# Attention followed by routed experts on one core: the first batch's keys fetched ahead of its queries, in fewer transfers, and the second batch's q and k issued later

## Chip, core and metric

The kernel runs on one core of a Trainium2 chip. The metric is the device time of one execution in microseconds (us). Engines are named as in the profile: PE (matrix multiplication; PEld are its weight loads), DVE (vector), ACT (activation), POOL (GpSimd) and SP (which here only issues transfers). POOL and SP each issue transfers to a queue of their own, q0 for POOL and q1 for SP; both are served by the core's 16 DMA engines.

## What is computed

The attention takes q, k and v of shape (8 batches, 8 heads, 576 rows, 64). It is the sum of two attentions: one on rows averaged in fours (144 by 144 scores, repeated back to 576 rows) and one in a band of three rows either side. Its output, seen as 4608 rows of 512, goes through eight experts; each row goes to one of them.

```python
out_d = sm_attn(q_d, k_d, v_d)            # rows averaged in fours
mask = np.abs(pos[:, None] - pos[None, :]) < 4
out_local = softmax(where(mask, scale * q @ k.T, -1e9)) @ v
x = (np.repeat(out_d, 4, axis=2) + out_local)  # as (4608, 512)
e_idx = argmax(x @ w_gate)
out[mask_e] = gate_w * eom * (relu(x @ w1[e]) @ w2[e])
```

## The kernel before

**Units.** Attention works in 32 units u0 to u31, four for each batch; a unit is two heads. q and k of a batch come in four slots, a slot being two neighbouring heads: 128 partitions of nine rows each. The transfer converts float32 to float16. Slots 0 and 1 are needed together by the first pair of units (w = 0: u0 and u1), slots 2 and 3 by the second (w = 1). The second batch's q and k serve u4 to u7, the third batch's u8 to u11.

**Loads.** `load_qk` (L436 to L448) makes one POOL task for q and one for k. For the first batch it is called three times, for slot 0, for slot 1 and for slots 2 and 3 (L864), so that POOL issues q, k, q, k, q, k; for each later batch it is called once with all four slots. Two buffers each for q and k hold two batches, so the third batch's loads wait until the first batch's slots have been transposed. `load_v` (L452) makes four SP transfers of 80 KB for each unit; each is 64 partitions of five runs of 64 numbers, so 320 pieces of 256 bytes. v has five buffers: u0 to u4 are issued without waiting, u5 needs u0's buffer. The v of u0 goes out at once; that of u1 waits for the first group of k transposes (the dependency "q and k go first", and L881). Behind the v of u4, SP issues eight small transfers of the gate's weights, wg (L402), and only then the v of u5.

**Front of the pipeline.** For a pair of units `prep` (L473) transposes k and then q on PE (L487, 18 instructions each, "Tk" and "Tq" here); DVE and ACT copy them out (L499; both groups of q on DVE). POOL then adds neighbouring rows: ks and kd from k (L512, L521), qs and qd from q (L512, L515). For the first pair, POOL does each unit by itself: ks, kd, qs, qd of u0, then of u1; after that come ks, kd, qs, qd of w = 1. Behind these, POOL makes constants for the gate (`c_gate`, L410 to L417), and DVE has a task `c_rev` (L420 to L427) that reads them. DVE runs its instructions in program order, and `c_rev` stands ahead of the first unit's normalisation.

**A unit.** `means_v` (L531) averages v on PE (L380, called VD), ACT copies the means. `scores` (L549) makes the averaged scores (L560, DS) and the band scores (L573 and L583, LS) on PE, and ACT takes exponentials. `values` (L592) multiplies by v: V1 (L609, averaged), V2 (L618, sums), V3 (L630, band). ACT makes reciprocals (L643, L638, L646), DVE multiplies (L653, and L660 with L664: M1), POOL adds the two attentions (L670). In PE's order VD(u1) stands ahead of V1(u0), and VD(u5) ahead of LS(u3). A few products without use (`fill`, L1008) are put on PE where the planner sees a gap; four of them stand ahead of V1(u1) and write a tile that M1(u0) reads.

**What orders the work.** Every piece is a task with a planned duration, a slot number and a weight from a table. `order` (L118) simulates the engines and yields one sequence; `late` (L165) walks it and holds a task back until its dependencies, its buffers and, where set, the task named in its `behind` have been emitted. `behind` places tasks in an engine's queue by hand; for the head of the kernel these stand in L880 to L888:

```python
    for u in range(1, NU):
        for t in vb[u][1]:
            t.behind = st[0]["tk"]
    t_wg.behind = vb[3][1][-1]
    st[1]["e21"][1].behind = st[0]["e20"][0]
    st[2]["e21"][0].behind = st[1]["e20"][1]
    t_cg.behind = st[2]["e20"][0]
```

In these names `e20` is POOL's qs with qd and `e21` its ks with kd, indexed by the unit of the pair; `qb[b]["loads"][0]` lists the loads of slots 0 and 1, q first and k last. Before the change the second batch's loads have no `behind`: POOL issues q of the second batch after the first few constants and k after the band masks, both before any work on the first batch. Each engine runs its own queue in order, and semaphores hold it where data is missing.

Of the kernel before, what the change touches and what calls it, by code (L numbers as in the profile page):

```python
# [51 lines left out]
def _ap(t, ap_list, extra_off=0):  # L52
    return bass.AP(tensor=t.tensor, offset=t.offset + extra_off, ap=ap_list)
# [27 lines left out]
class Plan:  # L81
# [9 lines left out]
    def add(self, kind, slot, eng, dur, fn, deps=(), uses=(), mode=None, lat=0.0, dma=0.0):  # L91
        t = Task(kind, slot, eng, dur, fn, [d for d in deps if d is not None], list(uses), mode, lat, dma)
        for b in t.uses:
            b.users.append(t)
        for d in t.deps:
            d.next.append(t)
        self.tasks.append(t)
        return t
# [105 lines left out]
def kernel(  # L204
# [11 lines left out]
    nc = tc.nc  # L216
    B, H, S, D = q.shape
# [213 lines left out]
    qb, vb = {}, {}  # L431
# [4 lines left out]
    def load_qk(b, s0=0, s1=NP):  # L436
        if b not in qb:
            qb[b] = {"bufs": [Buf(r_qk[0]), Buf(r_qk[1])], "loads": {}}
        for i, src in enumerate((q, k)):
            buf = qb[b]["bufs"][i]  # L440

            def fn(buf=buf, src=src):
                nc.gpsimd.dma_start(buf.tile[:, s0:s1, :],
                                    _ap(src[b, 2 * s0], [[9 * D, 128], [2 * S * D, s1 - s0], [1, 9 * D]]))
            t = add("qk"[i] + "b" if b else "qk0", NP * (b - 1) if b else s0 - 9, "POOL", 0.84, fn, uses=[buf],
                    dma=0.95 * (s1 - s0))
            for s in range(s0, s1):
                qb[b]["loads"].setdefault(s // 2, []).append(t)  # L448
# [20 lines left out]
    st = {}  # L469
# [381 lines left out]
    def weights(e, part=None):  # L851
# [3 lines left out]
        for i, w in enumerate((moe_w1, moe_w2)):  # L855
# [4 lines left out]
            elif part // 2 == i:  # L860
                c = slice(part % 2 * n // 2, (part % 2 + 1) * n // 2)
                nc.gpsimd.dma_start(wts[e][i][:, c], src[:, c])

    for s in ((0, 1), (1, 2), (2, 4)):  # L864
        load_qk(0, *s)
    for b in range(1, B):
# [18 lines left out]
    for t in st[2]["tq"]:  # L885
        t.behind = st[0]["ds"]
    st[2]["e21"][0].behind = st[1]["e20"][1]
    t_cg.behind = st[2]["e20"][0]  # L888
    t_w = {}
    for e in range(3):  # L890
# [172 lines left out]
    def tiles():  # L1063
        return (sbF.tile([128, 4, 128 * CAPJ], F16, tag="xgT", name="xgT"),
                sbF.tile([128, NG, 128 * CAPJ], F16, tag="hs", name="hs"),
                sbF.tile([128, CAPJ, Dm], F32, tag="y", name="y"))

    with tc.manual_schedule():
# [8 lines left out]
        for e in range(E):  # L1077
            w1sb, w2sb = wts[e]
            xgT, hs, y = xts[e]
# [10 lines left out]
            for j in range(nj):  # L1090
                col = CAPJ * (E - 1 - e) + parts[e][1] + j
                down(xgs[e], hs, y, j, w2sb, sidx[:, col:col + 1], True)
                k = 1 if nj > 2 else 2
# [10 lines left out]
    with tc.If(v_most > 0):  # L1104
# [12 lines left out]
        for e in range(E):  # L1117
# [4 lines left out]
            with tc.For_i(0, n_more, 1):  # L1122
# [13 lines left out]
                xgT, hs, y = tiles()  # L1136
# [34 lines left out]
```

## Time and profile before

| | |
|---|---|
| median of 3 runs | 387.89 us (384.99 to 389.81) |
| the profiled execution | 390.27 us |
| its span, first to last instruction | 388.5 us |
| PE busy in the span | 333.7 us (86%) |
| POOL busy | 236.1 us (61%) |
| ACT, DVE busy | 199.9 us (51%), 194.6 us (50%) |
| mean granted clock of PE | 0.975 |

The profiled execution took 390.27 us, of which 388.5 us lie between its first and its last instruction and 1.77 us around them. Times of rows are counted from the first instruction. A PE that is busy by the profile is not PE at its peak, since matmuls are pipelined. A granted clock of 1.00 is the upper of PE's two levels (2.4 GHz), 0.50 the lower (1.2 GHz).

### The profile page before, as it was taken

Reading aid. Unit: us, or ns where it says so; the run is one execution under the profiler, and the core shown is the slowest. Engines: PE = TensorE matmul, PEld = TensorE weight load, DVE = VectorE, ACT = ScalarE, POOL = GpSimd, SP = SyncE. Lnnn points to the kernel's source line nnn. Section 1 sums busy time; section 2 is a strip of 40 time slices with the busy share of each in tenths; the row PEclk is TensorE's granted clock in tenths of the full one; section 3 lists DMA queues with packets and bytes.
Section 4 is the critical chain, followed back from the end, with each engine's and each line's share of the span. In section 5 each row is a group of like instructions: output and inputs, shape, how many; then the busy total and the mean of one; then the engine's idle time right before and its main releaser. Section 6 shows DMA issues by size and latency. Waiting matters only on the chain.

```text
span 388.5 us, 13050 instructions
## 1 busy us (share of the span) xinstructions
PE 333.7 (86%) x5542; PEld 236.7 (61%) x5542; DVE 194.6 (50%) x505; ACT 199.9 (51%) x421; POOL 236.1 (61%) x295
## 2 busy tenths in 40 slices
PE   1685998998778877888887889999999999999991
PEld 1564776786667665666675666555756565666650
DVE  4634357778466675657783767322334232323210
ACT  1346676687567775746776544234333334333431
POOL 8867396778475677556667361356766766752322
PEclk9999899999989999889999999999999999999997
DMA  8949359969797999857495131434999999980212
GB/s 137 211 75 188 71 103 153 191 146 165 149 173 125 166 179 165 157 105 136 96 167 109 36 93 47 137 119 111 194 253 259 242 264 224 236 241 29 94 56 81
DMA packets 75237, 57.12 MB, mean 147 GB/s; under 512 B 46493, under 2 KB 67485, under 8 KB 75168
## 3 DMA queue, kind: packets, MB, share of 16 engines
q0 software_dynamic: 26272, 40.92, 53.8%
q1 hardware_dynamic: 48896, 15.26, 18.3%
q8 instruction: 45, 0.74, 0.8%
q14 instruction: 24, 0.20, 0.2%
HBM read 68.21 MB, written 15.22 MB: 215 GB/s over the span
## 4 chain that ended last, share of the span: by engine, by line
PE 56%; issue 13%; DMA 9%; ACT 9%; DVE 5%; POOL 4%; SPq 1%; POOLq 0%; DVEq 0%; ACTq 0%
PE PL L609 8%; PE U L1048 6%; PE Y L1058 6%; PE S L618 4%; PE PL L974 4%; DMA v<-in_v_dram 4%; PE PL L630 4%; POOL out_dram L909 3%; PE PL L960 3%; PE T L487 3%; PE T L380 3%; PE T L834 3%; PE T L710 3%; DMA xg<-hx_xs,gidx 3%; PE S L560 2%
## 5 line engine op out<-in xcount | busy, mean ns | idle before, releaser
L1058 PE MATMUL Y<-w,hs 128*128 128x512 f16 x248 | 57.3, 379 | 0.0
L909 POOL DMA_INDIRECT out_dram<-y,sidx x31 | 30.7, 990 | 39.7 <-ACT y L1060 22.1
L1048 PE MATMUL U<-xgT,w 128*128 128x320 f16 (+1 forms) x384 | 51.9, 295 | 0.4 <-DVE hs L1053 0.4
L670 POOL TENSOR_TENSOR x<-xl,xd 128x576 f16<-128x576 f32 x32 | 39.8, 1247 | 18.8 <-DVE xl L664 15.1
L1053 DVE TENSOR_SCALAR hs<-U 128x320 f16<-128x320 f32 (+1 forms) x52 | 24.6, 476 | 51.6 <-PE U L1048 40.2
L1048 PEld LDWEIGHTS <-w 128*128 128x128 f16 x416 | 40.6, 98 | 16.0 <-issue 1.8
L1060 ACT ACTIVATE y<-Y,xg 128x512 f32<-128x512 f32 x31 | 21.2, 687 | 45.6 <-PE Y L1058 31.6
L904 POOL DMA_INDIRECT xg<-hx_xs,gidx x31 | 31.5, 1017 | 14.2 <-issue 7.9
L1058 PEld LDWEIGHTS <-hs 128*128 128x128 f16 x248 | 23.6, 98 | 24.3
L1051 ACT ACTIVATE hs<-U 128x320 f16<-128x320 f32 (+1 forms) x52 | 21.9, 424 | 28.0 <-PE U L1048 27.1
L609 PE MATMUL PL<-e,vd 64*128 64x144 f32 x384 | 35.6, 320 | 0.0
L521 POOL TENSOR_TENSOR kd<-ks 64x192 f16<-64x192 f32 x64 | 32.4, 523 | 2.3
L487 PE MATMUL T<-id,qk 128*64 128x128 f16 x576 | 25.8, 237 | 9.3 <-POOL gfirst L356 6.1
L512 POOL TENSOR_TENSOR ks<-kT 128x576 f32<-128x576 f16 (+1 forms) x17 | 18.6, 1093 | 24.5 <-ACT kT L499 22.2
L630 PE MATMUL PL<-e,v 64*64 64x57 f32 (+1 forms) x1280 | 26.9, 220 | 6.9 <-issue 5.6
L499 DVE COPY qT<-T 128x640 f16<-128x640 f16 (+1 forms) x32 | 24.4, 773 | 14.6 <-PE T L487 6.5
L630 PEld LDWEIGHTS PL<-e,v 64*64 64x64 f32 x1280 | 24.0, 134 | 12.3 <-issue 6.4
L609 PEld LDWEIGHTS PL<-e,vd 64*128 64x128 f32 x384 | 28.0, 201 | 5.0 <-issue 2.4
L487 PEld LDWEIGHTS <-qk 128*64 128x64 f16 x576 | 19.6, 119 | 12.9 <-DMA qk<-in_k_dram 8.5
L380 PE MATMUL T<-v,pv 128*32 128x64 f32 (+1 forms) x512 | 19.4, 257 | 9.3 <-DMA v<-in_v_dram 3.7
L618 PE MATMUL S<-e,on_l 64*64 64x291 f32 x256 | 23.4, 437 | 4.0 <-ACT e L565 2.8
L646 ACT ACTIVATE r<-r 128x726 f32<-128x726 f32 x32 | 25.9, 809 | 0.5
(158 smaller groups left out, 646.3 us busy)
## 6 DMA issues: line engine op xcount, KB each, us to landing
v<-in_v_dram SPq DMA_DIRECT2D x128, 80.0 KB, 5.1
w<-in_moe_w_dram POOLq DMA_DIRECT2D x10, 1024.0 KB
w<-in_moe_w_dram POOLq DMA_DIRECT2D x12, 512.0 KB
hx_xs<-xh SPq DMA_DIRECT2D x8, 578.2 KB, 4.9
qk<-in_q_dram POOLq DMA_DIRECT2D x7, 576.0 KB
qk<-in_k_dram POOLq DMA_DIRECT2D x7, 576.0 KB
xg<-hx_xs,gidx POOLq DMA_INDIRECT x31
out_dram<-y,sidx POOLq DMA_INDIRECT x31
```

The source lines that it names most:

```text
L380: nc.tensor.matmul(o if last else o.rearrange("p (b d) -> p b d", b=2), lhsT=pv[:, s + 4 * last, :], rhs=rhs(NB - 1 if last else s, h, 1 i ...
L487: t = nc.tensor.transpose(t16[64 * y:64 * y + 64, 128 * (c - c0):128 * (c - c0) + 128], src.tile[:, 2 * (w % 2) + y, D * c:D * c + D], id16)
L521: nc.gpsimd.tensor_tensor(o.rearrange("p b (s x) -> p b s x", s=2), _ap(t, [t.ap[0], [114, 3], [58, 2], [2, 32]]), _ap(t, [t.ap[0], [114, ...
L609: nc.tensor.matmul(o, lhsT=vd.tile[r, blk, D - D * h:3 * D - D * h], rhs=x, start=(blk == 0), stop=(blk == 2), skip_group_check=True)
L618: nc.tensor.matmul(p[64 * h:64 * h + 64, par, 0:WC], lhsT=on_l[r, :], rhs=et[r, h, 0:WC], start=True, stop=True, skip_group_check=True)
L630: nc.tensor.matmul(p[64 * h:64 * h + 64, par, c0:c1], lhsT=vbuf.tile[r, g, h, :], rhs=et[r, h, c0:c1], start=(g == 0), stop=True, skip_gro ...
L646: lx = add("LX", u, "ACT", 0.73, lambda: nc.scalar.activation(r_.tile, r_.tile, AF.Exp, scale=-1.0), deps=[l1, l2], uses=[r_])
L670: nc.gpsimd.tensor_tensor(x16.tile[:, hp, :].rearrange("p (n m) -> p n m", m=4), xl.tile[:, hp, :].rearrange("p (n m) -> p n m", m=4), _bc ...
L904: nc.gpsimd.indirect_dma_start(out=dst, out_offset=None, in_=xs_dram.ap()[0:rows, :], in_offset=bass.IndirectOffsetOnAxis(ap=idx, axis=0), ...
L909: ins = nc.gpsimd.indirect_dma_start(out=out, out_offset=bass.IndirectOffsetOnAxis(ap=idx, axis=0), in_=y, in_offset=None, bounds_check=N ...
L1048: nc.tensor.matmul(pu[:, 0:c1 - c0], lhsT=w1sb[:, c, 128 * f:128 * f + 128], rhs=xgT[:, c, c0:c1], start=(c == 0), stop=(c == 3))
L1058: nc.tensor.matmul(py, lhsT=hs[:, f, 128 * j:128 * j + 128], rhs=w2sb[:, f, :], start=(f == 0), stop=(f == NG - 1))
```

## The change

The first batch's six transfers become four, each of two slots: k of slots 0 and 1, q of slots 0 and 1, k of slots 2 and 3, q of slots 2 and 3. The six tasks remain; the first four issue one transfer each from a list, and the last two issue nothing. The second batch's k is placed on POOL's queue behind u0's qs and qd, its q behind u1's qs and qd. Nothing else is changed.

```diff
@@ load_qk, L442 @@
             def fn(buf=buf, src=src):
-                nc.gpsimd.dma_start(buf.tile[:, s0:s1, :],
-                                    _ap(src[b, 2 * s0], [[9 * D, 128], [2 * S * D, s1 - s0], [1, 9 * D]]))
+
+                i, c0, c1, x = src is k, s0, s1, buf
+                if not b:
+                    if not early:
+                        return
+                    i, c0 = early.pop(0)
+                    c1, x = c0 + 2, qb[0]["bufs"][i]
+                    for y in qb[0]["bufs"]:
+                        if y.tile is None:
+                            y.tile = y.ring.make()
+                nc.gpsimd.dma_start(x.tile[:, c0:c1, :],
+                                    _ap((q, k)[i][b, 2 * c0], [[9 * D, 128], [2 * S * D, c1 - c0], [1, 9 * D]]))
@@ before the calls of load_qk, L864 @@
+    early = [(i, s0) for s0 in (0, 2) for i in (1, 0)]
@@ the list of behind, L887 @@
     st[2]["e21"][0].behind = st[1]["e20"][1]
+    qb[1]["loads"][0][-1].behind = st[0]["e20"][0]
+    qb[1]["loads"][0][0].behind = st[1]["e20"][1]
     t_cg.behind = st[2]["e20"][0]
```

## Rows read from the trace of the kernel before

**Rows 1.** Chain of waits, first 48 us: start, us, what.

```profile
3.14 5.44 DMA qk<-in_k_dram
...
11.38 8.06 DMA v<-in_v_dram
...
31.71 6.76 DMA v<-in_v_dram
```

**Rows 2.** Timeline of PE, 0 to 48: start, us, what, count, [idle before <-releaser].

```profile
6.11 0.31 PE L487 MATMUL T<-id,qk 128*64 128x128 f16 x1 [6.11 <-POOL gfirst L356]
...
10.28 1.17 PE L487 MATMUL T<-id,qk 128*64 128x128 f16 x18 [0.49 <-DVE kT L499]
...
25.58 0.67 PE L1008 MATMUL PL<-pv 128*128 128x76 f32 x4 [1.15 <-DVE xl L664]
26.18 1.01 PE L609 MATMUL PL<-e,vd 64*128 64x144 f32 x12
...
27.41 0.69 PE L487 MATMUL T<-id,qk 128*64 128x128 f16 x18
...
37.76 0.38 PE L380 MATMUL T<-v,pv 128*32 128x128 f32 x2 [1.56 <-DMA v<-in_v_dram]
...
39.40 0.46 PE L573 MATMUL S<-mk,id 64*64 64x291 f16 x4
...
40.05 1.81 PE L609 MATMUL PL<-e,vd 64*128 64x144 f32 x12
```

**Rows 3.** Timeline of POOL, 9 to 28 us.

```profile
9.20 0.76 POOL L443 DMA_DIRECT2D qk<-in_k_dram  x1
...
12.67 0.66 POOL L512 TENSOR_TENSOR qs<-qT 128x288 f32<-128x288 f16 x1 [0.23 <-DVE qT L499]
...
16.50 0.42 POOL L515 TENSOR_TENSOR qd<-qs 128x144 f16<-128x144 f32 x1
...
22.68 0.14 POOL L413 IOTA rev_i<- 128x8 int32 x1
...
26.76 0.77 POOL L443 DMA_DIRECT2D qk<-in_q_dram  x1
```

**Rows 4.** Timeline of DVE, 9 to 26 us.

```profile
9.41 0.82 DVE L499 COPY kT<-T 128x640 f16<-128x640 f16 x1 [1.30 <-PE T L487]
...
16.43 1.45 DVE L499 COPY qT<-T 128x640 f16<-128x640 f16 x2 [0.84 <-PE T L487]
22.85 0.19 DVE L421 CAST rev<-rev_i 128x48 f32<-128x48 int32 x1 [4.97 <-POOL rev_i L413]
...
23.93 0.62 DVE L653 TENSOR_TENSOR xd<-PL,r 64x144 f32<-64x144 f32 x2 [0.23 <-PE PL L1008]
...
25.36 0.16 DVE L664 TENSOR_TENSOR xl<-PL,r 128x6 f32<-128x6 f32 x1
```

**Rows 5.** Timeline of SP, 9 to 40 us: start, us from first to last, count.

```profile
9.40 0.60 SPq L460 DMA_DIRECT2D v<-in_v_dram  x1
...
23.37 3.17 SPq L406 DMA_DIRECT2D wg<-in_moe_w_gate_dram  x4
...
29.32 10.60 SPq L460 DMA_DIRECT2D v<-in_v_dram  x12
```

**Rows 6.** DMA queues from 9 to 13 us: packets, MB, share of 16 engines.

```profile
q0 software_dynamic: 745, 0.83, 120.9%
```

**Rows 7.** The same from 31 to 34.5 us, and from 34.5 to 38.

```profile
q1 hardware_dynamic: 468, 0.02, 19.0%
...
q1 hardware_dynamic: 2310, 0.56, 94.0%
```

**Rows 8.** Two stretches: us, busy PE PEld DVE ACT POOL, PEclk, DMA share, GB/s.

```profile
34.90:38.20 3.30, 0.77 (x13) 0.36 (x10) 1.53 (x4) 0.97 (x2) 2.71 (x3) 1.00 1.21 211
38.50:41.50 3.00, 2.90 (x50) 2.63 (x50) 0.00 (x0) 0.66 (x1) 0.00 (x0) 0.50 0.53 116
```

**Rows 9.** POOL's issues by L443, whole span: count, ns min/median/max.

```profile
L443 POOL DMA_DIRECT2D qk<-in_k_dram x10: 576/762/783, 2.1 to 143.8; - x10
```

## The prediction

> **What bounds the kernel now.** I read the page first: PE is busy for 86% of the span, and PE's line is thin only in its first slices. So I took the chain of waits for the first 48 us [rows 1]. The reader is to see that three transfers carry it: k until 3.14 + 5.44 = 8.58, v until 11.38 + 8.06 = 19.44 (the v of u1), v again until 31.71 + 6.76 = 38.47 (the v of u5). Behind that the units run on PE, ACT and DVE, and the change touches nothing there. Then the timelines of the engines, to see what is late next where a wait goes. On PE [rows 2] the first transposition starts at 6.11, when the first two slots (q, k) have landed; it goes on at 8.58, with the fourth slot. Four `fill` products at 25.58 wait for DVE, and V1(u1) at 26.18 stands behind them. VD(u5) waits at 37.76, and LS(u3) behind it starts at 39.40. POOL [rows 3] runs from qs of u0 at 12.67 to the constant rev_i at 22.68, and DVE [rows 4] waits 4.97 us for that constant before it may normalise u0 (23.93, done at 25.52). SP [rows 5] issues v from 9.40, wg from 23.37, and only at 29.32 the v of u5.
>
> **Step 1, the first four slots.** From the second to the fourth slot it took 8.58 - 6.11 = 2.47 us, 1.23 a slot. k is now the first two slots, q the next two: k complete at 6.1, q at 8.6. Tk starts 2.5 us earlier. Tq started at 10.28 because its buffers had to be copied out first [rows 2]; these are now free 2.5 us sooner, so Tq starts with its data, at 8.6: 1.7 earlier. Bounds for q's landing: a slot's time earlier (7.4), if a transfer of two slots has less to do than two of one, or a slot's time later (9.8), if the v of u1 takes a share. I take 8.6, the row itself. The two issues that fall away hide behind the landing; they stood in front of POOL's constants, which wait for nothing critical.
>
> **Step 2, POOL and DVE.** qs of u0 follows Tq by 12.67 - 10.28 = 2.4 us [rows 2, 3], so it starts at 11.0. From there POOL has no gap above 0.3 us until rev_i, and the change puts two issues into this run: the second batch's k behind qd of u0, its q behind qd of u1 (the one at 16.50). Ten issues of this line took 0.58 to 0.78 us [rows 9]; the moved one took 0.76 at 9.20 [rows 3]. So 1.7 saved, 1.5 given back: rev_i at 22.5, 0.15 earlier. Where these issues stood before they cost nothing: POOL waited for k's copies behind them. DVE then starts u0 at about 23.6, 0.35 earlier (0.2 of it because the `fill` that it waited for is early by then). V1(u1) and the sum of u0 on POOL, behind which the third batch's q is issued (26.76), gain the same 0.35. For the price of an issue the ends are 0.58 and, if one is held for DVE's longest run of copies at this place (1.45 at 16.43 [rows 4]), 2.2; I take 0.76, ten rows against a supposition.
>
> So the wait for the v of u1 goes, but it buys little. That v is issued at 6.9 instead of 9.40. Between 9 and 13 us queue q1 moved nothing at all while q0 moved 745 pieces [rows 6]: v lands once q0 is empty. A slot has 128 pieces, so the first batch's other four slots take 512/186 = 2.8 us and q0 is empty at about 10.5; the second batch's k is issued at 12.2 at the earliest. The v of u1 lands near 13, and PE gets through V1 to V3 of u0 nearly 3 us earlier, only to meet the four `fill` products, which wait for DVE until 25.2. Late next is POOL's run, not v. The second batch's data has a wide margin: k issued at 12.2, q at 16.0, 512 pieces each, landed by 18 and 22; Tk of u4 stands at 27.41.
>
> **Step 3, the v of u5.** SP starts 2.5 us earlier, so wg goes at 20.9 and the v of u5 at 26.8. The third batch's q and k, however, start only 0.35 earlier: issued at 26.4, flowing near 27.8. Before, u5's v stood wholly behind them. Between 31 and 34.5 q1 moved 468 pieces of 43 bytes on average (0.02 MB): those were wg's, not v's of 256 bytes. Behind them 2310 pieces went in 3.5 us, 660 a us [rows 7]. Now wg's pieces and the first v transfer (320 pieces) are gone before the burst: 788 pieces less ahead, 1.2 us, so u5's v lands at 38.47 - 0.35 - 1.2 = 36.9, and LS(u3) starts near 37.5: 1.9 earlier. At the other end nothing waits: VD(u5) follows VD(u4), which ended at 37.76 - 1.56 = 36.20 [rows 2], so LS(u3) starts at 36.20 - 0.35 + 0.5 = 36.4, 3.0 earlier (the 0.93 from landing to LS(u3) was at the clock's lower level, below; 0.5 at the upper). That needs SP to run faster. Its sixteen v issues took (23.37 - 9.40)/16 = 0.87 us each where a free one takes 0.60 [rows 5], since the queue stood still from 9 to 13; part of that goes too. At the low end v comes as late as now and only 0.35 is left. I take 2.4, between the two cases that follow from rows.
>
> **Step 4, the clock.** From 34.9 to 38.2 PE had work for only 0.77 us; then its granted clock was 0.50 from 38.5 to 41.5 [rows 8]. Twelve products took 1.81 us there, 1.01 at 26.18 [rows 2], so 2.9 us of busy PE cost 2.9 x (1 - 1.01/1.81) = 1.3 too much. With the wait of step 3 mostly gone I expect no fall, and count 1.1, since ACT bounds the end of that stretch. Ends: 0 and 1.3.
>
> **Sum.** 2.4 + 1.1 = 3.5 us (the 0.35 is inside the 2.4). The profiled execution took 390.27, 388.5 of them span; it becomes 386.8. It lay 2.4 above the median of the runs shown, so I put the same 3.5 to the median: 387.89 - 3.5 = 384.4 us.
>
> **Rivals.**
> A, the clock falls earlier instead. PE runs out of work near 21.6 and has none until 25.2; before, that gap was 1.15 [rows 2]. For a fall: the 3.3 us with 0.77 of work ahead of the one in [rows 8]. Against: that stretch was emptied by several waits. At the lower level PE loses 1.2 behind 25.2; VD(u5) then finds its v landed, LS(u3) is 1.8 early, and nothing is saved on the clock: 386.1.
> B, the v of u5 stays behind the third batch. For it: q1's silence in [rows 6], which would hold three of its four transfers; against: wg's pieces are out of the way. 0.35 is left: 387.5.
> C, an issue is held by DVE. For it: both issues now stand where DVE builds its masks and copies q of the next pair. Against: ten issues, none above 0.78 [rows 9]. At 1.45 more each, V1(u1) comes 2.55 later than before, LS(u3) at 36.4 + 2.9 = 39.3, and the clock's 1.1 is all: 386.7.
> The Trainium skill, SBUF — State Buffer, section "SBUF: two separate sides", says that GpSimd cannot write a transfer's descriptors while DVE runs a two-port operation, and gives 620 ns alone against some 3100 beside one. With its figure the two issues would cost 4.7 us more, and the time would be an estimated 388.5. The rows speak against it: the issue at 9.20 took 0.76 with DVE's copy of 0.82 beside it from 9.41 [rows 3, 4].
> D, slower: the clock falls at 25 and stays down. Place: PE from V1(u1) on, where each us at the lower level loses 0.44. Price: the one fall seen lasted 3 us; four times that, 12 us, loses 5.3, against 3.0 from the v of u5 and 1.1 from the later fall, of which nothing more can be had: 1.2 slower, 389.1. It decides from 9.3 us. Against it: the fall in [rows 8] ended while PE was busy.
>
> **How the numbers follow.** Forecast 0.48 (with step 3 anywhere from 1.9 to 3.0), A 0.25, B 0.12, C 0.08, D 0.04, a cause that I don't see 0.03. Low end: 3.0, 1.3 of clock and 1.2 from an early q make 5.5, or 382.4; the runs shown differ by several us, so I go 1.5 lower, 380.9. High end: B at 387.5 and D at 389.1, cut at 388.8. A difference of 2%, 7.8 us, is about what a measurement of this kernel can tell from no change. No case gains that much by its steps; 0.10 for faster allows for stalls further on that shift with the start, 0.04 for slower is D, 0.86 is left within 2%.
>
> **What would show it.** Tk of u0 whole at 6.1, Tq at 8.6; POOL's qs of u0 at 11.0, two issues of 0.76 in the run, rev_i near 22.5; VD(u1) without a wait for v; `fill` ahead of V1(u1) waiting over 3 us for DVE; v of u5 issued by 26.8; LS(u3) between 36.4 and 37.5; granted clock 1.00 from 38 to 42. Wrong if rev_i comes over 1 us later than 22.7, if VD(u5) still waits to 38, or if the clock is 0.50 behind 25.

## The result, and the profile after

The changed kernel took 386.12 us in the median of 20 runs (380.20 to 392.55), the kernel before on the same chip 387.31 in the median of 20 (383.51 to 390.10). The ratio is 0.9899, 95% interval 0.9862 to 0.9936; it leaves out disturbed runs, ten of the twenty of the changed kernel among them, and so is further from 1 than the two medians are (0.997). Applied to the 387.89 us shown ahead of the prediction it gives 384.0; predicted were 384.4. Two later comparisons gave 0.9896 (0.9853 to 0.9939) and 0.9884 (0.9812 to 0.9957), where the plain medians stand at 0.989 and 0.992. So about 1%, or 4 us, is won. The working behind the number held less well.

The profiled execution took 380.91 us (span 379.2, mean granted clock 0.979). It is 9.4 us shorter than the one before, but the head, the first 46 us or so, accounts for 1.8 us of that. Line numbers after the change are 10 higher from L453 to L680 (Tk and Tq L497, LS L583 and L593, V1 L619, M1 L670 and L674) and 13 higher at `fill`, L1021; L380, L406 and L413 have not moved. In a count like x4 an f32 product stands twice: the four `fill` records are two products.

PE's timeline after the change (start, us, what, count, idle before and its releaser), which answers to [rows 2]:

```profile
6.70 1.17 PE L497 MATMUL T<-id,qk 128*64 128x128 f16 x18 [6.70 <-DMA qk<-in_k_dram]
8.55 1.17 PE L497 MATMUL T<-id,qk 128*64 128x128 f16 x18 [0.68 <-DMA qk<-in_q_dram]
...
15.79 0.64 PE L380 MATMUL T<-v,pv 128*32 128x128 f32 x16 [0.29 <-DVE qT L509]
16.35 1.01 PE L619 MATMUL PL<-e,vd 64*128 64x144 f32 x12
...
25.05 1.14 PE L1021 MATMUL PL<-pv 128*128 128x76 f32 x4 [3.98 <-DVE xl L674]
26.12 1.81 PE L619 MATMUL PL<-e,vd 64*128 64x144 f32 x12
...
33.78 1.01 PE L619 MATMUL PL<-e,vd 64*128 64x144 f32 x12
...
38.18 0.53 PE L380 MATMUL T<-v,pv 128*32 128x128 f32 x14 [0.17 <-DMA v<-in_v_dram]
38.64 0.32 PE L583 MATMUL S<-mk,id 64*64 64x291 f16 x4
...
39.04 1.01 PE L619 MATMUL PL<-e,vd 64*128 64x144 f32 x12
...
43.91 1.01 PE L619 MATMUL PL<-e,vd 64*128 64x144 f32 x12
```

PE's timeline of the kernel before, V1(u2) and V1(u4), which did not stand ahead of the prediction:

```profile
31.86 1.01 PE L609 MATMUL PL<-e,vd 64*128 64x144 f32 x12
...
45.72 1.01 PE L609 MATMUL PL<-e,vd 64*128 64x144 f32 x12
```

Read V1 unit by unit. V1(u0) is at 16.35 against 20.04, without a wait for v. V1(u1) is at 26.12 against 26.18: everything won is lost in the 3.98 us in which the four `fill` records wait for DVE. V1(u1) takes 1.81 instead of 1.01, which is the lower clock, and V1(u2) is 1.9 us *later* than before. VD(u5) then still waits for v, LS(u3) is at 38.64 against 39.40, and V1(u3) runs at the upper clock, where it had 1.81 before. V1(u4) is 45.72 - 43.91 = 1.8 us earlier. That is the gain of the head in this pair.

POOL's timeline after, which answers to [rows 3]:

```profile
10.94 0.66 POOL L522 TENSOR_TENSOR qs<-qT 128x288 f32<-128x288 f16 x1 [0.42 <-DVE qT L509]
...
12.08 0.80 POOL L453 DMA_DIRECT2D qk<-in_k_dram  x1
...
15.90 0.77 POOL L453 DMA_DIRECT2D qk<-in_q_dram  x1
...
22.50 0.14 POOL L413 IOTA rev_i<- 128x8 int32 x1
...
26.23 0.76 POOL L453 DMA_DIRECT2D qk<-in_q_dram  x1
```

DVE's, which answers to [rows 4]:

```profile
22.67 0.19 DVE L421 CAST rev<-rev_i 128x48 f32<-128x48 int32 x1 [6.30 <-POOL rev_i L413]
```

SP's (start, us from first to last, count), which answers to [rows 5]:

```profile
7.48 12.34 SPq L470 DMA_DIRECT2D v<-in_v_dram  x16
20.72 2.55 SPq L406 DMA_DIRECT2D wg<-in_moe_w_gate_dram  x4
...
27.00 2.79 SPq L470 DMA_DIRECT2D v<-in_v_dram  x4
```

The two moved issues stand in POOL's run at 0.80 and 0.77 us, rev_i comes at 22.50, and DVE now waits 6.30 us for it instead of 4.97. The v of u5 goes out at 27.00 instead of 29.32. The chain of waits shows what this was worth, beside [rows 1]:

```profile
1.36 5.30 DMA qk<-in_k_dram
...
29.10 8.95 DMA v<-in_v_dram
```

The last of its four transfers lands at 29.10 + 8.95 = 38.05, against 38.47. The first, issued at 27.00, landed 7.5 us later, at 34.5; the other three, issued between 27.6 and 29.1, needed 8.9 to 9.7 us and landed between 37.3 and 38.05. In the view of the load's line those are, for the first and for the other three:

```profile
DMA to landing us min/median/max: 7.5/7.5/7.5
...
DMA to landing us min/median/max: 8.9/9.3/9.7
```

In the kernel before all four needed 6.8 to 8.0 us and landed between 37.3 and 38.5. So one transfer of four landed 2.8 us earlier, between the third batch's q (26.23 + 6.2 = 32.4) and its k (26.98 + 10.1 = 37.1), and three hardly earlier. Queue q1 after the change, in the stretches 9 to 13, 28 to 31, 31 to 34.5 and 34.5 to 38, which answers to [rows 6, 7]:

```profile
q1 hardware_dynamic: 2010, 0.49, 65.7%
...
q1 hardware_dynamic: 144, 0.00, 6.6%
...
q1 hardware_dynamic: 426, 0.11, 23.1%
...
q1 hardware_dynamic: 2234, 0.54, 90.3%
```

From 9 to 13 us q1 moves 2010 pieces where it moved none. From 31 to 34.5 its 426 pieces now have 0.11 MB, v's size, so wg is out of the way. But none of v's moved from 28 to 31, where 144 pieces had less than 0.01 MB. From 34.5 on q1 carries as much as before. Windows (us, busy PE PEld DVE ACT POOL, PEclk, DMA share, GB/s), the last two beside [rows 8]:

```profile
25.10:31.00 5.90, 5.90 (x69) 4.73 (x71) 0.83 (x1) 0.82 (x3) 2.63 (x3) 0.50 0.68 87
34.90:38.20 3.30, 2.49 (x86) 1.57 (x79) 2.07 (x6) 2.76 (x7) 2.88 (x4) 1.00 1.04 183
38.50:41.50 3.00, 3.00 (x87) 2.38 (x85) 1.19 (x3) 1.58 (x5) 1.29 (x2) 1.00 0.42 93
```

The fall of the clock has moved: 0.50 from 25.1 to 31, and 1.00 from 38.5 to 41.5, where it was 0.50.

### The profile page after: what moved, and what is told of

Read it like the earlier page. It is cut to its first block, busy times and chain, and to the rows that moved or that the text cites. A ratio compares the mean times of both kernels' runs of the same rounds, so it can differ in the third digit from the quotient of the medians.

```text
span 379.2 us, 13049 instructions
## 1 busy us (share of the span) xinstructions
PE 330.7 (87%) x5542; PEld 235.1 (62%) x5542; DVE 195.4 (52%) x505; ACT 200.4 (53%) x421; POOL 235.8 (62%) x293
## 4 chain that ended last, share of the span: by engine, by line
PE 58%; issue 11%; ACT 10%; DMA 9%; DVE 4%; SPq 3%; POOL 3%; POOLq 0%; DVEq 0%; ACTq 0%
PE U L1061 8%; PE Y L1071 8%; PE PL L619 7%; DMA v<-in_v_dram 5%; PE PL L973 4%; PE PL L987 4%; PE S L628 4%; PE T L497 3%; PE T L844 3%; PE PL L640 3%; PE T L720 3%; POOL out_dram L922 3%; DMA xg<-hx_xs,gidx 3%; PE T L380 3%; SPq L470 3%
## 5 line engine op out<-in xcount | busy, mean ns | idle before, releaser
L680 POOL TENSOR_TENSOR x<-xl,xd 128x576 f16<-128x576 f32 x32 | 39.8, 1247 | 13.0 <-DVE xl L674 10.6
L1064 ACT ACTIVATE hs<-U 128x320 f16<-128x320 f32 (+1 forms) x52 | 22.1, 425 | 27.6 <-PE U L1061 27.5
L522 POOL TENSOR_TENSOR ks<-kT 128x576 f32<-128x576 f16 (+1 forms) x17 | 18.6, 1092 | 27.4 <-ACT kT L509 25.1
L619 PE MATMUL PL<-e,vd 64*128 64x144 f32 x384 | 34.5, 315 | 0.0
L531 POOL TENSOR_TENSOR kd<-ks 64x192 f16<-64x192 f32 x64 | 32.4, 523 | 2.3
L497 PE MATMUL T<-id,qk 128*64 128x128 f16 x576 | 25.6, 238 | 7.5 <-DMA qk<-in_k_dram 6.7
L640 PE MATMUL PL<-e,v 64*64 64x57 f32 (+1 forms) x1280 | 26.0, 223 | 5.6 <-issue 4.3
L619 PEld LDWEIGHTS PL<-e,vd 64*128 64x128 f32 x384 | 27.4, 198 | 4.8 <-issue 2.2
L653 ACT ACTIVATE r<-PL 64x144 f32<-64x144 f32 x64 | 18.3, 286 | 17.6 <-PE PL L619 13.9
L628 PE MATMUL S<-e,on_l 64*64 64x291 f32 x256 | 23.6, 440 | 4.0 <-ACT e L575 2.9
L497 PEld LDWEIGHTS <-qk 128*64 128x64 f16 x576 | 19.6, 120 | 11.0 <-DMA qk<-in_k_dram 6.7
L656 ACT ACTIVATE r<-r 128x726 f32<-128x726 f32 x32 | 25.9, 808 | 0.5
```

Of the source, the lines that this page charges most:

```text
L497: t = nc.tensor.transpose(t16[64 * y:64 * y + 64, 128 * (c - c0):128 * (c - c0) + 128], src.tile[:, 2 * (w % 2) + y, D * c:D * c + D], id16)
L531: nc.gpsimd.tensor_tensor(o.rearrange("p b (s x) -> p b s x", s=2), _ap(t, [t.ap[0], [114, 3], [58, 2], [2, 32]]), _ap(t, [t.ap[0], [114, ...
L619: nc.tensor.matmul(o, lhsT=vd.tile[r, blk, D - D * h:3 * D - D * h], rhs=x, start=(blk == 0), stop=(blk == 2), skip_group_check=True)
L628: nc.tensor.matmul(p[64 * h:64 * h + 64, par, 0:WC], lhsT=on_l[r, :], rhs=et[r, h, 0:WC], start=True, stop=True, skip_group_check=True)
L640: nc.tensor.matmul(p[64 * h:64 * h + 64, par, c0:c1], lhsT=vbuf.tile[r, g, h, :], rhs=et[r, h, c0:c1], start=(g == 0), stop=True, skip_gro ...
L656: lx = add("LX", u, "ACT", 0.73, lambda: nc.scalar.activation(r_.tile, r_.tile, AF.Exp, scale=-1.0), deps=[l1, l2], uses=[r_])
```

## The experiments

Theory one is this reading: two things hold the head, DVE's wait for rev_i (with the lower clock behind it) and the v of u5. Each instant given is that of one profiled execution of the kernel named, and a ratio is to the kernel before on the same chip.

**The changed kernel again (e1_again), and a third time (e10_after_again).** No edit.

> The changed kernel once more, to tell which parts of the 9.4 us between the two profiled executions belong to the change. Theory 1 (only the head of the kernel is changed, about 1.8 us): V1(u1) again near 26.1 at the lower clock, V1(u4) again 1.5 to 2.0 us earlier than 45.72, but the distance from V1(u4) to the last V1 (168.3 us in the first profile of it, 173.8 before) differs from profile to profile by several us. Theory 2 (the change also spares waits further on): that distance is again within 1 us of 168.3.

Measured: 0.9896 (0.9853 to 0.9939); V1(u1) at 25.9 with 1.81, V1(u4) at 43.76, and from there to the last V1 172.0 us. That is 3.7 more than in the first profile of the same kernel, as theory one has it.

> The changed kernel a third time, for comparison with the kernel with both edits on the same chip: ratio 0.990 to the kernel before, V1(u1) at 25.9 to 26.1 with 1.81, V1(u4) at 43.8 to 43.9. Theory one (the head's gain of 1.8 us is all that the change brings, the rest is spread of the later part): the ratio lies nearer to 0.995 than to 0.990. Theory two (the change gives something in the later part too): 0.990 again, as in both comparisons so far.

Measured: 0.9884 (0.9812 to 0.9957), theory two's number; V1(u1) at 26.49 with 1.81 and V1(u4) at 44.18, both 0.3 to 0.4 us later than expected. The gain repeats three times at 1.0 to 1.2%, and so does the head: V1(u4) at 43.91, 43.76, 44.18.

**The kernel before again (e5_before_again), and a third time (e11_before_third).** No edit; the kernel before as a kernel of its own.

> The kernel before once more, for a second profile of it. Theory 1 (the change acts on the head alone, 1.8 us at V1(u4); the rest of the 9.4 us between the first two profiled executions is what one execution differs from another further on): V1(u4) again within 0.5 us of 45.7, and from there to the last V1 about 172 us, as in the four profiles of changed heads other than the first (171.2 to 172.0), not 173.8. Theory 2 (the change also spares some 2 us further on): V1(u4) at 45.7 and the distance again at 173.5 or above.

Measured: 1.0197 (0.9977 to 1.0416), from four runs: the interval holds 1, and that is all that they tell. PE's timeline:

```profile
19.29 1.37 PE L380 MATMUL T<-v,pv 128*32 128x128 f32 x16 [2.01 <-DMA v<-in_v_dram]
20.59 1.81 PE L609 MATMUL PL<-e,vd 64*128 64x144 f32 x12
...
47.13 1.01 PE L609 MATMUL PL<-e,vd 64*128 64x144 f32 x12
```

VD(u1) waits 2.01 us for the v of u1, and here the clock falls behind that wait: V1(u0) takes 1.81. In the first profile V1(u0) ran at the upper level after two waits of VD(u1), 1.06 and 0.66 us. V1(u4) is 1.4 us later than in that profile, 1.35 of which were lost by V1(u1) already (27.53 against 26.18); both theories had V1(u4) near 45.7. From V1(u4) to the last V1 it is 177.3 us, which is on theory two's side. So the wait that the change removes costs more in some executions than in the one that the prediction read.

> The kernel before once more, as a kernel of its own on the same chip: what two measurements of one and the same kernel differ by. Theory one expects a ratio of 1.000 with an interval that holds 1, V1(u4) at 45.7 to 47.1 and a distance from V1(u4) to V1(u31) between 172 and 178 us (two looks so far: 173.8 and 177.4). If the distance is again above that of the changed kernel beside it (168.3, 171.9), theory two gains: something of the change reaches beyond the head.

Measured: 0.9985 (0.9938 to 1.0033) from 12 runs, so with this many runs one kernel agrees with itself within 0.7%; with four it came out at 1.02. None of the three intervals of the changed kernel, from 6 to 20 runs, holds 1. The profile shows V1(u0) again with 1.81 behind waits of 1.45 and 1.71 us for v, and V1(u4) at 49.93, well outside the 45.7 to 47.1 that were expected; but it is of the longest of the twelve runs (392.33 us) and stands for less than the other two. The distance to the last V1 is 173.2 us, above the three of the changed kernel, which is on theory two's side too.

**The new order alone (e2_order_only).** The two lines that ask for the second batch later are left out:

```diff
-    qb[1]["loads"][0][-1].behind = st[0]["e20"][0]
-    qb[1]["loads"][0][0].behind = st[1]["e20"][1]
```

> k first, two slots a transfer, but the second batch's q and k issued where they were before. Theory 1 (POOL's run up to rev_i is late next): POOL gets 1.5 us back, rev_i near 21.0, DVE begins u0 near 21.9, V1(u1) near 24.5 with a gap on PE of under 3 us; v of u1 now queues behind 16 slots and lands near 17 to 18, just late enough to show. V1(u4) as early as in the changed kernel or up to 1 us earlier. Theory 2 (the second batch standing in the queue is what held the first units): VD(u1) waits until 19 as before, V1(u1) at 26, V1(u4) within 0.5 us of 45.7.

Measured: 1.0044 (0.9963 to 1.0124). PE's timeline:

```profile
20.73 0.86 PE L380 MATMUL T<-v,pv 128*32 128x128 f32 x14 [3.60 <-DMA v<-in_v_dram]
21.52 1.81 PE L619 MATMUL PL<-e,vd 64*128 64x144 f32 x12
...
48.12 1.01 PE L619 MATMUL PL<-e,vd 64*128 64x144 f32 x12
```

Tk starts as early as in the changed kernel, but the v of u1 is starved: all sixteen slots stand on q0. From 12 to 16 us q0 and q1 moved 578 pieces each (0.65 and 0.14 MB), and the last transfer of that v, issued at 8.78, landed 11.46 us later, at 20.24. An earlier start bought a longer wait, the clock fell in V1(u0), and V1(u4) is at 48.12. rev_i did come at 21.24, as theory one expected, but DVE then had to wait for V1 to V3 of u0, which the v of u1 held back: theory two's wait, and longer. The new order alone is worth nothing here.

**The later request alone (e3_move_only).** The kernel before with only these two lines added:

```diff
+    qb[1]["loads"][0][-1].behind = st[0]["e20"][0]
+    qb[1]["loads"][0][0].behind = st[1]["e20"][1]
```

> The old six transfers in the old order, but the second batch's q and k behind qd of u0 and of u1. Theory 1: qs of u0 stays at 12.7, POOL's run gets 1.5 us longer, rev_i near 24.2, DVE begins u0 near 25.0, V1(u1) near 27.4 and at the lower clock, V1(u4) 0.5 to 2 us later than 45.72, although VD(u1) no longer waits for v. Theory 2: VD(u1) without its wait makes V1(u4) earlier than 45.72 by 1 us or more.

Measured: 0.9958 (0.9909 to 1.0007). PE's timeline:

```profile
17.74 0.87 PE L380 MATMUL T<-v,pv 128*32 128x128 f32 x16
...
27.09 1.13 PE L1010 MATMUL PL<-pv 128*128 128x76 f32 x4 [4.05 <-DVE xl L664]
28.15 1.81 PE L609 MATMUL PL<-e,vd 64*128 64x144 f32 x12
...
45.84 1.01 PE L609 MATMUL PL<-e,vd 64*128 64x144 f32 x12
```

VD(u1) starts at 17.74 without a wait, so it is this half that frees the v of u1. But the two issues now stand in POOL's run without an earlier start to pay for them: DVE gets rev_i at 24.7, `fill` waits 4.05 us, V1(u1) is 2 us later than before and at the lower clock. V1(u4) comes level with the first profile of the kernel before (45.84 against 45.72) and not later, since V1(u3) then runs at the upper clock (1.01). In these profiles neither half brings V1(u4) forward by itself: the order brings the start, the later request takes the wait away. The ratios say less, for the interval of this half overlaps that of the changed kernel on the same chip (0.9853 to 0.9939).

**rev off DVE's path (e4_rev_late).** `c_rev` goes behind M1(u0), so that u0 no longer waits for POOL's constants:

```diff
-    t_cg.behind = st[2]["e20"][0]
+    t_cg.behind = st[2]["e20"][0]; t_rev.behind = xb[0]["mul"][0]
```

> The changed kernel with DVE's task that reads the gate's constants put behind the normalisation of u0. Theory 1 (that task and POOL's run behind it held PE from 21 to 25 and brought the lower clock): DVE begins u0 near 20.5, V1(u1) near 22.7 in about 1.0 us, clock 1.00 from 25 to 29, the third batch's q issued near 23.8; v of u5 still behind it, landed near 35; V1(u4) near 40 instead of 43.9, and the time 3 to 4 us shorter than the changed kernel's. Theory 2 (v is what bounds, whatever DVE does): v of u5 lands at 38 as before, V1(u4) within 0.5 us of 43.9.

Measured: 390.06 us in the median of 4 runs (386.37 to 394.51), beside 393.96 of the kernel before; too few for a ratio. PE's timeline:

```profile
23.06 1.01 PE L619 MATMUL PL<-e,vd 64*128 64x144 f32 x12
...
35.44 0.38 PE L380 MATMUL T<-v,pv 128*32 128x128 f32 x2 [2.84 <-DMA v<-in_v_dram]
...
37.03 1.66 PE L619 MATMUL PL<-e,vd 64*128 64x144 f32 x12
...
43.41 1.01 PE L619 MATMUL PL<-e,vd 64*128 64x144 f32 x12
```

V1(u1) comes 3 us earlier and at the upper clock. The third batch's q is issued at 24.50 instead of 26.23, though, ahead of the whole v of u5 (27.28), which now makes PE wait 2.84 us and brings the lower clock there. Of 3 us at V1(u1) and 5 at V1(u2) 0.5 is left at V1(u4). Expected were 40 by theory one and 43.9 by theory two: the number is theory two's, though v landed near 36 and not at 38.

**The v of u5 ahead of wg (e6_wg_late).** The gate's weights go behind the v of u5 instead of that of u3:

```diff
-    t_wg.behind = vb[3][1][-1]
+    t_wg.behind = vb[5][1][-1]
```

> The changed kernel with the gate's weights wg issued behind the v of u5 instead of ahead of it. Theory 1 (v of u5 was late because SP issued wg first and the third batch's q and k got into the queue before it): v of u5 issued near 20.7, landed by 26, VD(u5) without a wait for v; V1(u1) unchanged near 26.1 at the lower clock; LS(u3) near 37.7 instead of 38.6, V1(u4) near 43.0. Theory 2 (v of u5 does not matter once the clock has fallen): V1(u4) within 0.3 us of 43.9.

Measured: 0.9981 (0.9910 to 1.0052), the medians 387.94 against 393.98. No verdict: against the same runs of the kernel before, that kernel itself came out at 1.0197 (e5_before_again). PE's timeline:

```profile
25.93 1.81 PE L619 MATMUL PL<-e,vd 64*128 64x144 f32 x12
...
33.59 1.01 PE L619 MATMUL PL<-e,vd 64*128 64x144 f32 x12
...
36.23 1.13 PE L380 MATMUL T<-v,pv 128*32 128x128 f32 x32
...
42.56 1.01 PE L619 MATMUL PL<-e,vd 64*128 64x144 f32 x12
```

All of the v of u5 is issued before 23.4, ahead of the third batch (26.04). VD(u4) and VD(u5) run as one group, without a wait; LS(u3) is at 37.29 and V1(u4) 1.35 us earlier than in the changed kernel. That is the price of what is left of the wait for v, as long as the wait for DVE stays.

**Both edits (e7_both, then e9_both_again).** The edits of the last two together. (In the second expectation "the flips" are `c_rev`, "the flipped weights" are wg, and its first figure, 11.7 us, is the distance of no two profiles; the sums behind it go by 5.9 and 7.7.)

> The changed kernel with both: DVE's task behind the normalisation of u0, and wg behind the v of u5. Theory 1 (each of the two waits hid the other): V1(u1) near 23.1 at the upper clock, VD(u5) without a wait, LS(u3) near 33 to 34, V1(u4) near 38.5, and the time 4 to 5 us shorter than the changed kernel's, 8 to 9 us (2.2%) shorter than the kernel before. Theory 2 (a third wait stands close behind): V1(u4) not before 42.

Measured: 0.9895 (0.9749 to 1.0041) from four runs, which holds 1. PE's timeline:

```profile
22.46 1.01 PE L619 MATMUL PL<-e,vd 64*128 64x144 f32 x12
...
38.04 1.01 PE L619 MATMUL PL<-e,vd 64*128 64x144 f32 x12
```

Alone, the edits were worth 0.5 and 1.35 us at V1(u4); together 43.91 - 38.04 = 5.9, with LS(u3) at 32.77 and no wait for v in VD(u5). Neither wait can be priced by taking it away alone: each covered the other.

> The kernel with both edits again (the slot's group and the flips late, the flipped weights' load late), beside the changed kernel and the kernel before on one chip. If the 11.7 us that the look at it showed between the two V1(u4) (38.0 against 49.7 would be no gain; the looks were 38.0, changed 43.9, before 45.7) reach the end, it is 5.9 us, 1.5%, under the changed kernel and 7.7 us, 2.0%, under the kernel before: ratio 0.980. If what is won at the head is given back by a lower clock behind it (176.4 us from V1(u4) to V1(u31) in the first look, against 168.3 and 171.9 of the changed kernel), it is level with the changed kernel, 0.990. V1(u4) is expected at 38.0 again, and V1(u1) at 22.5 with 1.01.

Measured: 378.69 us in the median of 6 runs, the kernel before 386.36, ratio 0.9756 (0.9687 to 0.9825); the changed kernel on the same chip 0.9884. Of the versions run this is the fastest, and the ratio is that of a gain which reaches the end. Its profile, of the longest of the six runs, shows V1(u1) at 23.25 and V1(u4) at 39.38, 0.8 and 1.3 us later than expected (against 44.18 of the changed kernel beside it that is 4.8), and the next wait, of VD(u7), in PE's timeline:

```profile
47.75 0.53 PE L380 MATMUL T<-v,pv 128*32 128x128 f32 x14 [1.75 <-DMA v<-in_v_dram]
```

Behind it V1(u5) is at 49.77, only 1.4 us ahead of the changed kernel's 51.19; the first profile of both edits has no such wait and V1(u5) at 45.33.

**No fill ahead of V1(u1) (e8_no_fill).** The four records of `fill` that wait for DVE are left out, and the six behind VD(u2) with them (they write nothing that is read):

```diff
-            live[0] = True
+            live[0] = u > 0
```

> The changed kernel without the ten products without use that stand around u0 and u1 (six behind VD(u2), four ahead of V1(u1)). Theory 1 (the four hold PE until DVE is done with u0, though V1(u1) does not need that): V1(u1) starts near 21.8 instead of 26.1; PE waits a little later for DVE instead; the clock stays up or falls for less time; v of u5 still lands at 38, V1(u4) near 43.5. Theory 2 (PE was held by data): V1(u1) starts at 25 or later.

Measured: one run, 393.79 us. PE's timeline:

```profile
36.95 0.61 PE L380 MATMUL T<-v,pv 128*32 128x128 f32 x2 [6.57 <-DMA v<-in_v_dram]
```

V1(u1) came at 21.28, near what was expected; V1(u4) was expected at 43.5 and came at 47.05. The v of u5 does not come earlier with it (issued from 26.62, last landed at 38.81), so PE waits for 6.57 us in one piece, and V1(u3) then takes 1.81. So theory one is right about what held V1(u1), and wrong about what comes of it: PE further ahead of the same v lost 3 us at V1(u4) where 0.4 were to be gained.

**More work on PE in the wait for DVE (e12_warm).** On top of the late wg, 25 products without use behind LS(u1), in a tile that nothing reads:

```diff
+        if u == 1:
+            band = fn
+            def fn():
+                band()
+                w = pv.rearrange("p g n -> p (g n)")
+                for _ in range(25):
+                    nc.tensor.matmul(PL_s[1][:, 0, WC + SD:WC + SD + 76], lhsT=w[:, 0:128], rhs=w[:, 0:76], start=True,
+                                     stop=True, skip_group_check=True)
```

> The kernel with the late load of the flipped weights, and 25 more products without use on PE behind LS(u1), in a tile that nothing reads: 3.6 us of work in the 4.8 us in which PE otherwise waits for DVE. Theory one (the price of that wait is the lower clock behind it): V1(u1) still at 25.9, held by the same four products, but with 1.01 in place of 1.81; V1(u2) at 31.7 in place of 33.6, LS(u3) at 35.4 in place of 37.3, and V1(u4) at 40.7 in place of 42.6, unless the v of u5, which had then landed by 36.2, is late again: then LS(u3) at 36.5 and V1(u4) near 41.7. Theory two (the 1.9 us at V1(u2) are DVE's and ACT's, which start u0 and u1 late either way): V1(u1) 1.01, but V1(u2) still at 33.6 and V1(u4) at 42.6.

Measured: 383.22 us in the median of 6 runs, ratio 0.9884 (0.9820 to 0.9947). PE's timeline:

```profile
20.73 5.81 PE L603 MATMUL PL<-pv 128*128 128x76 f32 x50
...
26.91 1.01 PE L628 MATMUL PL<-e,vd 64*128 64x144 f32 x12
...
32.59 1.01 PE L628 MATMUL PL<-e,vd 64*128 64x144 f32 x12
...
41.79 1.01 PE L628 MATMUL PL<-e,vd 64*128 64x144 f32 x12
...
50.58 0.53 PE L380 MATMUL T<-v,pv 128*32 128x128 f32 x14 [2.52 <-DMA v<-in_v_dram]
```

(V1 is L628 in this kernel, the products L603, two records each; the profile is of the longest of the six runs.) They took 5.81 us instead of 3.6, so V1(u1) is 1.0 later than without them, and V1(u2) and V1(u4) come about 1 us later than expected. From V1(u1) to V1(u2) it is 32.59 - 26.91 = 5.68 us, against 33.59 - 25.93 = 7.66 without them (e6_wg_late), and 5.68 in the kernel before. All other profiles agree: where `fill` stands and V1(u1) takes 1.01, the distance is 5.67 or 5.68; in the five where it takes 1.81, it is 7.16 to 7.67. So the price of the lower clock behind the wait is 1.5 to 2.0 us, and it is the clock's, not DVE's or ACT's: DVE begins u0 as late as without the products (23.50 against 23.27). What is won shows at V1(u4) (41.79 against 42.56, in spite of the later start) and meets the wait of VD(u7): V1(u5) is at 52.39, where the late wg alone has it at 49.84.

## Why the prediction came out as it did

**Step 1 and step 2, the instants: right.** Tk at 6.70 (6.1 predicted: the transfer of both slots of k landed at 1.36 + 5.30 = 6.66; nothing was lost by it, as Tq then waited for q), Tq at 8.55 (8.6), qs at 10.94 (11.0), the issues 0.80 and 0.77 (0.76), rev_i at 22.50 (22.5), u0's normalisation at 23.45 (23.6), V1 to V3 of u0 almost 4 us earlier and lost again in front of `fill`, which waits 3.98 (over 3). Rival C fell: the issue at 12.08 took 0.80 with copies of DVE beside it from 12.09. The figure of some 3100 ns that the Trainium skill gives beside a two-port operation of DVE (SBUF — State Buffer, "SBUF: two separate sides") did not show; whether these copies are such operations no view tells, so the rule itself is not tested here.

**Step 2, "the wait for the v of u1 goes, but it buys little": too low in some executions.** In the profile that I read, V1(u0) kept the upper clock. In e5_before_again it did not, and V1(u4) was 1.4 us later; nor in e11_before_third. One profiled execution shows the wait, but not the spread of what it costs.

**Step 3, the v of u5: the term was mis-sized.** 2.4 us were predicted at LS(u3), 0.76 came. The issue at 27.00 (26.8) was right, and so was it that wg goes ahead; the third batch's q went out 0.53 earlier (26.23 against 26.76), not 0.35. The error is the line "788 pieces less ahead, 1.2 us": v was to land at 36.9 and landed at 38.05, 0.42 earlier than before, so nothing came of the 1.2. I let v follow as a stream, in the order of issue. But the first transfer, issued at 27.00, was not gone before the burst: its pieces moved from 31 on, beside the third batch's. And from 31 to 38 q1 moved 426 + 2234 = 2660 pieces, twice the 1280 of u5's v, whose last transfer landed only then: the v of u6, issued from 31.8, moved beside it. The other three transfers of u5 were issued at 27.6 to 29.1, as the third batch began to flow (17 pieces of q0 from 26 to 28, 404 from 28 to 31), and landed within about 0.4 us of where they had. That is rival B's mechanism, for three of the four transfers, as its "for it" said; where all four go out well ahead of the third batch (e6_wg_late), VD(u5) does not wait.

**Step 4, the clock: its saving came, beside a loss.** From LS(u3) to V1(u4) it was 45.72 - 39.40 = 6.32 us and is 43.91 - 38.64 = 5.27: 1.05 saved, 1.1 predicted. But the clock also fell behind the wait for DVE, rival A, to which I gave 0.25, and at 2.0 us, not 1.2. In the changed kernel that loss lies mostly under the late v: with V1(u1) at the upper clock, V1(u2) comes 5 us earlier and V1(u4) only 0.5 (e4_rev_late).

**The sum.** Predicted for the head were 3.5 us; this pair of profiles shows 0.76 + 1.05 = 1.8. The timed gain is about 4. Between e5_before_again and the changed kernel the head differs by 47.13 - 43.91 = 3.2, so part of what is missing may be the spread of step 2. The rest lies behind V1(u4) and is open. In the first pair V1(u11) is still 1.8 us earlier (89.81 against 91.59) and the last V1 7.3 (212.21 against 219.52). From V1(u4) to the last V1 the kernel before took 173.8, 177.3 and 173.2 us, the changed kernel 168.3, 172.0 and 169.8. That looks like something spared further on, but the order alone and the later request alone, neither clearly faster than the kernel before, took 171.8 and 171.9, and the first profile of both edits 176.4. The profiles differ there in idle time of PE with no releaser ("issue") and in the granted clock (0.93 to 0.98 from 46 to 220 us); that these make the difference no run shows.

So the time was right and the sum behind it was not: 384.0 against 384.4 is in good part luck. Of the three signs of being wrong that the prediction named two came, VD(u5) waiting to 38.18 and the clock at 0.50 behind 25. Rival A's fall of the clock and rival B's late v, to which I gave 0.25 and 0.12 as cases by themselves, came together. What made up for them, the spread of step 2 and a gain behind the head, stands in no term of it.

## What to carry to other kernels

Price a wait by taking away its neighbours too: two edits worth 0.5 and 1.35 us at V1(u4) alone gave 5.9 together (4.8 in a second pair of profiles), and the timed ratio went from 0.988 to 0.976. A load that is wanted early gains by moving the transfers that compete with it, not only by starting sooner: the order alone gave 1.004, the later request alone 0.996, both 0.990. When PE gets ahead and then waits, add the slower clock behind the wait to its price; here it took back 1.5 to 2.0 us. And do not take a time that came true for a mechanism that did: look whether the signs named beforehand came.

## What the runs showed of the hardware

Transfers on q1 that are issued while q0's are under way can wait long: in the kernel before no piece from 9 to 13 us, while six were issued from 9.40 on; in e2_order_only as many pieces as q0's from 12 to 16 (578 to 578); and in the changed kernel 0.6 us between two issues (27.00 and 27.64) made a difference of 2.8 us in landing (34.5 against 37.3). Once they flow, they go piece for piece with q0's, and fast when q0 is empty: in the changed kernel q1 moved 288 pieces beside 286 from 32 to 34 us, and 1769 beside 41 from 35 to 37. What holds them at first is not separated by a run.

A busy PE did not get its clock back at once: from 25.1 to 31 us it was busy for all of 5.90 us at 0.50. In e10_after_again it was back sooner (1.00 from 30 to 32 us), with 7.16 us from V1(u1) to V1(u2). Nor is it the wait alone that tells what follows. Ahead of V1(u0) the kernel before waited 1.06 and 0.66 us in one profile and V1(u0) ran at the upper level; 2.01 us in another, and it ran at the lower. But the 18 transposes ahead of the wait (15.65 and 16.18) took 1.17 us in the first, the pace of the lower level (28.34 in the changed kernel, at 0.50), and 0.69 in the second. By these durations the clock rose in the first by the end of the wait, and in the second it had been up before and fell. The windows do not show it, for they give a granted clock of 1.00 ahead of the wait in both, so this is argued and not shown.
